# Moving weight sums and one layer norm in a fused attention and MLP kernel on one core

## The chip, the cores and the metric

One NeuronCore of a Trainium2 chip. Times are device microseconds of one execution; a run gives one time, and the median of the runs is compared. A profiled execution is a further run, taken by the hardware profiler.

## What is computed

The input x has 2048 rows of 1024. A layer norm is followed by linear attention with 32 heads of 32 and learned softmax features, and a second layer norm by a dense layer with 3584 hidden columns and a ReLU. All is fp32.

```python
xn = layernorm(x)
q, k, v = split(xn @ wqkv)                      # 32 heads of 32
pq, pk = q @ w_phi, k @ w_phi                   # per head
phi_q = concat(softmax(pq), softmax(-pq)); phi_k = the same of pk
o = (phi_q @ (phi_k.T @ v)) / (phi_q @ sum(phi_k) + 1e-6)
h = x + o @ wo
out = h + relu(layernorm(h) @ w1) @ w2
```

## The kernel before

Every large product is made of groups of three matmuls (`mm3`, lines 182 to 184): high half by high half, high by low, low by high. The halves come from splitting an fp32 tile: ScalarE copies the rounded high half, and VectorE or POOL (GpSimd) subtracts it to get the low half. One group of three is one *step*. The order of the work on each engine is the order in which the program writes it; nothing is reordered later. `when(step, f, ...)` puts a piece of side work right behind the given step of the matmul stream, so an engine's queue runs in order of steps, and an engine that waits holds all that stands behind it. Engines do not wait for the step itself, only for data and buffers, so a queue may also run ahead.

Steps 0 to 255 make keys and values of the first half of the rows in four slabs. Steps 256 to 383 make its queries in two slabs of eight row tiles: slab 0 in steps 256 to 319, slab 1 in 320 to 383. From step 328 on each item of eight steps is followed by two groups of four transposes of a normed row tile of the second half (`ln_turn`, L245). Steps 384 to 639 are keys and values of the second half, 640 to 767 its queries. Steps 768 to 1023 (`wo_first`) are the output projection, with the attention interleaved: unit u goes through products on POOL (`at_sums`, tile ez, L575), sums on VectorE (`at_reduce`, L581), scaling on POOL (`at_scale`, L603 for the first six units, L613 after them), a transpose on VectorE (`at_turn`, L619), and, two units at a time, 128 small matmuls (`at_num`, L633), whose four banks (two named tp, two ac) are then read by ScalarE and by VectorE (`at_low`, L651). In the late part `at_num` comes every 16 steps: ... 894, 910, 926, 942, 958. From step 1024 on the two dense products run.

*Weight units.* `Units` loads weights into six raw tiles (SP's queue, L324 to L337), splits each into a ring of ten (`advance`: ScalarE L125, then L129 on VectorE or POOL) and frees a place when its last step has passed. A slab has eight units. While slab 0 of the queries holds eight places, two of the next slab's units can be split; units 2 to 7 follow as steps 312 to 317 free places. Of these, units 2 and 5 are subtracted on VectorE, 3, 4, 6 and 7 on POOL.

*Weight sums.* The dense products use a seven-multiplication scheme on blocks of 2 by 2, which needs sums and differences of blocks of w1 and w2. They are made early, in 56 pieces. Each piece has a load of 512 KB (`t_load`, L352) seven or fifteen steps ahead, four subtractions on POOL at four consecutive steps (`t_sum`, L362, tiles 128x256), and a store of 512 KB six steps after the first (`t_store`, L365). Loads and stores go through SP's queue. Home 0 is a pair of buffers in the pool tsum, home 1 a pair in the pool fold (closed at step 256), home 2 the two xn tiles of the first layer norm.

*Layer norm ahead of the dense layers.* The kernel's name for it is LN2, and the halves of rows are its first and second part (b = 0 and 1); "first layer norm" in the change's title is b = 0. In each, four pairs of row tiles go through `ln_pair`, 40 steps apart from step 832 on (`wo0 + 64`): stage 0 loads both tiles (L215, tile xin, two buffers), 1 statistics (VectorE, L221), 2 the scale (POOL, L230 to L232), 3 the norm (ScalarE, L238), stages 4, 5 and 6 four transposes each into a tp bank (L245) with ScalarE's copy out (L247), stage 7 four more (L714), ScalarE's copy (L716) and two VectorE operations (L718, L719), stage 8 two POOL subtractions (L724, L725). `ln_store` then stores seven parts from SP (L734, 256 KB each, two to a step): x1's first half, two sums, x1's second half, x2's first half, a further sum (s4), x2's second half. SP's queue also has the attention loads (`at_load`, L543) and the loads and stores of the projection (L658, L687).

Of the kernel before, what the change touches and what calls it, by code (L numbers as in the profile page):

```python
# [140 lines left out]
def kernel(  # L141
# [47 lines left out]
    def do(n, k, f, *args):  # L189
        at[n, k].append((f, args))  # L190
# [663 lines left out]
    def item(gen, *args, keys):  # L854
        items.append((gen, args + (keys,)))
        steps.extend((k,) for k in keys)
        return len(items) - 1
# [11 lines left out]
    for b, tiles in enumerate(groups):  # L869
        for hf in range(2):  # L870

            pairs = b == 0 and hf == 0
            for j in range(0, 4, 2 if pairs else 1):
# [3 lines left out]
                for half in range(2):  # L877
                    n = item(wo_pair, tiles[j:j + 2], hf, half, keys=[("wo", hf, 4 * half + k // 2) for k in range(8)])
# [26 lines left out]
    def when(step, f, *args):  # L905

        if step < 8 * first_up:
            do(step // 8, step % 8, f, *args)
        else:
            do(first_up + (step - 8 * first_up) // 4, step % 4, f, *args)  # L910
# [4 lines left out]
    for t in range(1, NT):  # L915
        n = t - 1 if t < HT else q_n[1, t - HT] + 1
# [131 lines left out]

    LN2 = ((0, 9, 12, 17, 24, 25, 26, 27, 29, 36), (0, 18, 26, 32, 40, 42, 44, 46, 50, 60))
    wo0 = 8 * wo_first
    up0 = 8 * first_up
    for i in range(4):
        for stage in range(9):
            when(wo0 + 64 + 40 * i + LN2[0][stage], ln_pair, 0, i, stage)
            when(up0 + 60 + 68 * i + LN2[1][stage], ln_pair, 1, i, stage)
        for j in range(7):
            when(wo0 + 64 + 40 * i + LN2[0][9] + j // 2, ln_store, 0, i, j)
            when(up0 + 60 + 68 * i + LN2[1][9] + j, ln_store, 1, i, j)  # L1060
    assert wo_n[8, 0] + 10 < first_up

    def up_step(b, p, m):

        return up0 + 4 * (up_n[b, p, m] + 1 - first_up)

    for j, m in enumerate(UP):

        for g in range(2):
            step = up0 + (8 * j + (-62, -32)[g] if j < 4 else 6 * (j - 4) + 10 + 2 * g)  # L1070
# [4 lines left out]
            step = up_step(0, NP - 1, m) + 3 * j  # L1075
# [4 lines left out]
    for b in range(2):  # L1080
# [6 lines left out]


    sixth = 10, 19, 28, 37, 46, 55
    sums_at = [30, 39, 47, 55] + [64 * i + k for i in (1, 2, 3, 4) for k in sixth] + [332, 344, 356, 368] + \  # L1090
        [64 * i + k for i in (6, 7, 8, 9) for k in sixth]
    for n, (w, p, j) in enumerate((w, p, j) for w in (1, 2) for p in range(NP) for j in range(2)):
        step = sums_at[n]
        home = 0 if n % 4 < 2 or 236 < step < 400 else 1 if step < 256 else 2
        when(step - (7 if 256 < step < 400 else 15), t_load, w, p, j, home)
        for k in range(4):
            when(step + k, t_sum, (w, p, j), k)
        when(step + 6, t_store, w, p, j)

    for b in range(2):  # L1100
        for m in DOWN:
            n = down_n[b, m, NP - 1] + 1
# [111 lines left out]
```

## Time and profile before

| | |
|---|---|
| runs, median | 1895.59 us (3 runs, 1893.38 to 1896.5) |
| profiled execution, own time | 1895.65 us |
| its span, first to last instruction | 1893.9 us |
| mean granted TensorE clock | 0.998 |
| TensorE busy | 1879.6 us, 99% of the span |
| VectorE, ScalarE, POOL busy | 1048.3, 740.3, 975.9 us |
| DMA | 432.17 MB, mean 228 GB/s |
| POOL on weight sums (L362) | 176 + 48 subtractions, 144.6 + 41.6 us |

The span is cut into instructions by engine and line. PE is TensorE, DVE VectorE, ACT ScalarE, SP the queue that issues most DMAs. A timeline row has the start, the length, engine, line, operation, tiles, shapes and count; where the engine sat idle before it, brackets give the time and what ended the idle time. Matmuls are pipelined, so the listed length of one (0.39 us) is longer than the distance to the next; distances between starts tell the rate. The chain of waits that ended last is TensorE for 87% of the span and POOL for 7%.

### The profile page before, as it was taken

What the parts mean: (1) busy time and instruction counts of PE and PEld (TensorE: products, weight loads), DVE (VectorE), ACT (ScalarE), POOL (GpSimd) and SP (SyncE); (2) the same over time, 40 slices, a digit from 0 to 9 for tenths busy, and PEclk for the clock granted to TensorE, in tenths of its full rate; (3) what the DMA queues carried; (4) which work ended last, traced back from release to release, by engine and by line L of the source; (5) the groups of instructions that cost most, each with busy time, mean ns of one, the idle gap of its engine ahead of it and who ended that gap; (6) DMA issues with size and microseconds to landing.
All of it is one profiled execution on the core that took longest, in us unless ns stands there. A gap on an engine that the chain in (4) does not pass through costs nothing.

```text
span 1893.9 us, 31847 instructions
## 1 busy us (share of the span) xinstructions
PE 1879.6 (99%) x11640; PEld 1541.0 (81%) x11640; DVE 1048.3 (55%) x1687; ACT 740.3 (39%) x1258; POOL 975.9 (52%) x959
## 2 busy tenths in 40 slices
PE   9999999999999999999999999999999999999999
PEld 7777778888788787888888888888888888888887
DVE  6787668677689776555544563334333433343333
ACT  5322235222233122255454554444444444444442
POOL 4887743888936988323333222222344444444443
PEclk9999999999999999999999999999999999999999
DMA  7888687566555676796877986666677677767775
GB/s 224 289 292 290 228 284 253 187 197 199 186 195 175 205 243 211 251 271 212 276 229 244 296 271 218 184 194 204 216 238 218 197 233 237 240 212 219 215 215 179
DMA packets 292365, 432.17 MB, mean 228 GB/s; under 512 B 24048, under 2 KB 150000, under 8 KB 292208
## 3 DMA queue, kind: packets, MB, share of 16 engines
q1 hardware_dynamic: 275312, 413.36, 68.8%
q10 hardware_dynamic: 16896, 16.78, 2.6%
q8 instruction: 91, 1.49, 0.3%
q14 instruction: 66, 0.54, 0.1%
HBM read 292.68 MB, written 137.36 MB: 227 GB/s over the span
## 4 chain that ended last, share of the span: by engine, by line
PE 87%; POOL 7%; DMA 3%; issue 1%; DVE 1%; SPq 0%; ACT 0%; POOLq 0%; ACTq 0%
PE mm L182 22%; PE mm L183 22%; PE mm L184 22%; PE ac L182 4%; PE ac L184 4%; PE ac L183 4%; PE tp L182 2%; PE tp L184 2%; PE tp L183 2%; POOL ez L575 2%; POOL b L362 1%; PE tp L245 1%; DMA b<-in_w_dram 1%; POOL w L129 1%; POOL qe L613 1%
## 5 line engine op out<-in xcount | busy, mean ns | idle before, releaser
L129 POOL TENSOR_TENSOR w<-raw,w 128x512 fp32r<-128x512 f32 x353 | 468.2, 1328 | 733.1 <-ACT w L125 696.4
L125 ACT ACTIVATE w<-raw 128x512 fp32r<-128x512 f32 x686 | 409.6, 628 | 506.1 <-PE mm L184 249.9
L129 DVE TENSOR_TENSOR w<-raw,w 128x512 fp32r<-128x512 f32 x333 | 272.1, 818 | 525.2 <-ACT w L125 522.0
L182 PE MATMUL mm<-w,xT 128*128 128x512 f32 x768 | 306.4, 399 | 0.0
L183 PE MATMUL mm<-w,xT 128*128 128x512 f32 x768 | 301.5, 393 | 4.1 <-POOL w L129 3.8
L184 PE MATMUL mm<-w,xT 128*128 128x512 f32 x768 | 300.4, 391 | 0.0
L182 PE MATMUL mm<-hT,w 128*128 128x512 f32 x672 | 262.6, 391 | 0.0
L183 PE MATMUL mm<-hT,w 128*128 128x512 f32 x672 | 261.7, 389 | 0.5 <-DVE hT L754 0.5
L184 PE MATMUL mm<-hT,w 128*128 128x512 f32 x672 | 261.6, 389 | 0.0
L183 PEld LDWEIGHTS mm<-w,xT 128*128 128x128 f32 x768 | 144.9, 189 | 34.6 <-POOL w L129 5.6
L362 POOL TENSOR_TENSOR b<-b 128x256 f32<-128x256 f32 x176 | 144.6, 822 | 54.9 <-DMA b<-in_w_dram 44.7
L182 PEld LDWEIGHTS mm<-w,xT 128*128 128x128 f32 x768 | 144.9, 189 | 34.2 <-issue 2.9
L184 PEld LDWEIGHTS mm<-w,xT 128*128 128x128 f32 x768 | 144.9, 189 | 30.9
L182 PE MATMUL mm<-w 128*128 128x512 f32 x392 | 152.5, 389 | 0.0
L183 PE MATMUL mm<-w 128*128 128x512 f32 x392 | 152.5, 389 | 0.0
L184 PE MATMUL mm<-w 128*128 128x512 f32 x392 | 152.5, 389 | 0.0
L183 PEld LDWEIGHTS mm<-hT,w 128*128 128x128 f32 x672 | 126.2, 188 | 26.8 <-DVE hT L754 1.1
L184 PEld LDWEIGHTS mm<-hT,w 128*128 128x128 f32 x672 | 126.2, 188 | 26.3
L182 PEld LDWEIGHTS mm<-hT,w 128*128 128x128 f32 x672 | 126.2, 188 | 25.8
L182 PEld LDWEIGHTS mm<-w 128*128 128x128 f32 x392 | 73.6, 188 | 15.3
L184 PEld LDWEIGHTS mm<-w 128*128 128x128 f32 x392 | 73.6, 188 | 15.3
L183 PEld LDWEIGHTS mm<-w 128*128 128x128 f32 x392 | 73.6, 188 | 15.2
(170 smaller groups left out, 3143.9 us busy)
## 6 DMA issues: line engine op xcount, KB each, us to landing
raw<-t SPq DMA_DIRECT2D x224, 256.0 KB, 3.8
raw<-ad SPq DMA_DIRECT2D x196, 256.0 KB, 3.0
raw<-in_w_dram SPq DMA_DIRECT2D x168, 256.0 KB, 3.0
ad<-c SPq DMA_DIRECT2D x112, 256.0 KB, 3.5
b<-in_w_dram SPq DMA_DIRECT2D x44, 512.0 KB, 5.7
t<-b SPq DMA_DIRECT2D x44, 512.0 KB, 5.0
ad<-s SPq DMA_DIRECT2D x84, 256.0 KB, 4.1
ed<-qe ACTq DMA_DIRECT2D x32, 512.0 KB, 4.3
```

The costliest lines, as they stand in the source:

```text
L125: nc.scalar.activation(w[:, 0, :], raw[1], AF.Copy)
L129: eng.tensor_tensor(out=w[:, 1, :], in0=raw[1], in1=w[:, 0, :].bitcast(F32), op=ALU.subtract)
L182: pe.matmul(ps, a_hi, b_hi, start=first, stop=False, skip_group_check=more)
L183: pe.matmul(ps, a_hi, b_lo, start=False, stop=False, skip_group_check=more)
L184: pe.matmul(ps, a_lo, b_hi, start=False, stop=last, skip_group_check=more)
L245: pe.transpose(pt[:, k, :], xn[:, (4 * j + k) * P:(4 * j + k + 1) * P], ident)
L362: pool.tensor_tensor(out=tsum[*u, *out], in0=tsum[*u, *a], in1=tsum[*u, *b], op=ALU.subtract)
L575: pool.tensor_tensor(out=ez, in0=e_q[u].rearrange("p (i h) s f -> p i (h s f)", i=4)[:, 2 * j:2 * j + 2, :], in1=zb[:, q, None, 256 * r:25 ...
L613: pool.tensor_tensor(out=e, in0=e, in1=sd[:, :, None].to_broadcast([P, 32, 32]), op=ALU.mult)
```

## The change

Three edits to the table of side work. No operation is added or taken out.

1. Steps of the sums (`sums_at`). In steps 256 to 320: six sums at 266, 275, 284, 293, 302, 311 become four at 266, 276, 286, 296. In steps 320 to 384: four at 332, 344, 356, 368 become five at 332, 342, 352, 362, 372. All later sums keep their steps but each is made one place earlier in the list, and the last one goes to step 650, in the first query slab of the second half.
2. Homes of the buffers. Up to step 236 as before (0, 0, 1, 1); from there to 384 home 0; from 394 on the rotation 0, 0, 2, 2 is counted from the sum at 394 (`half_on`).
3. For the second pair (i = 1) of the layer norm with b = 0, stages 4 to 8 come five steps later and the stores one step later: with base step 872, stage 4 goes from 896 to 901, stage 7 from 899 to 904, stage 8 from 901 to 906, the stores from 908 to 909.

```diff
+    NEAR1 = 0, 9, 12, 17, 29, 30, 31, 32, 34, 37
     LN2 = ((0, 9, 12, 17, 24, 25, 26, 27, 29, 36), (0, 18, 26, 32, 40, 42, 44, 46, 50, 60))
...
     for i in range(4):
+        near = NEAR1 if i == 1 else LN2[0]
         for stage in range(9):
-            when(wo0 + 64 + 40 * i + LN2[0][stage], ln_pair, 0, i, stage)
+            when(wo0 + 64 + 40 * i + near[stage], ln_pair, 0, i, stage)
...
         for j in range(7):
-            when(wo0 + 64 + 40 * i + LN2[0][9] + j // 2, ln_store, 0, i, j)
+            when(wo0 + 64 + 40 * i + near[9] + j // 2, ln_store, 0, i, j)
...
     sixth = 10, 19, 28, 37, 46, 55
-    sums_at = [30, 39, 47, 55] + [64 * i + k for i in (1, 2, 3, 4) for k in sixth] + [332, 344, 356, 368] + \
-        [64 * i + k for i in (6, 7, 8, 9) for k in sixth]
+    sums_at = [30, 39, 47, 55] + [64 * i + k for i in (1, 2, 3) for k in sixth] + \
+        [266, 276, 286, 296, 332, 342, 352, 362, 372] + [64 * i + k for i in (6, 7, 8, 9) for k in sixth] + [650]
+    half_on = sums_at.index(64 * 6 + 10)
     for n, (w, p, j) in enumerate((w, p, j) for w in (1, 2) for p in range(NP) for j in range(2)):
         step = sums_at[n]
-        home = 0 if n % 4 < 2 or 236 < step < 400 else 1 if step < 256 else 2
+        home = (0, 0, 1, 1)[n % 4] if step < 236 else (0, 0, 2, 2)[(n - half_on) % 4] if n >= half_on else 0
         when(step - (7 if 256 < step < 400 else 15), t_load, w, p, j, home)
```

## The prediction

> **What bounds the kernel now.** I read the page's busy times first, then the list of TensorE's waits, then the timelines around each wait that the edited steps touch.
>
> ```profile
> PE 1879.6 (99%) x11640; PEld 1541.0 (81%) x11640; DVE 1048.3 (55%) x1687; ACT 740.3 (39%) x1258; POOL 975.9 (52%) x959
> ```
>
> The waits of TensorE (who, for whom: us in all, times, the longest):
>
> ```profile
> PE mm L183 <- POOL w L129: 3.8, 3, 3.2
> ...
> PE tp L245 <- DVE oT L651: 1.2, 1, 1.2
> ```
>
> TensorE is busy 99% of the span, and nothing in the diff removes a matmul. All that scheduling can give is TensorE's waits and what follows them. Two waits stand where the edit works: 3.2 us on POOL's split of a weight unit (L183, matmul with the unit's low half), and 1.2 us of a layer-norm transpose (L245) on VectorE.
>
> The first wait in TensorE's timeline (columns: start, us, engine, line, operation; idle time before it in brackets):
>
> ```profile
> 260.32 0.39 PE L182 MATMUL mm<-w,xT 128*128 128x512 f32 x1
> ...
> 264.40 0.39 PE L182 MATMUL mm<-w,xT 128*128 128x512 f32 x1
> 267.99 0.79 PE L183 MATMUL mm<-w,xT 128*128 128x512 f32 x1 [3.20 <-POOL w L129]
> ...
> 273.49 0.63 PE L182 MATMUL mm<-w,xT 128*128 128x512 f32 x1
> ...
> 274.71 0.40 PE L182 MATMUL mm<-w,xT 128*128 128x512 f32 x1
> ```
>
> From 260.32 to 264.40 there are six steps (18 matmuls): 4.08 / 18 = 0.227 us each, 0.68 a step. From 264.40 to 274.71 there are five steps (15 matmuls), which would take 3.40 us and took 10.31. So this stall costs **6.91 us**, twice its listed wait: the matmuls behind it last 0.63 instead of 0.39 until 274.
>
> What held POOL, by its timeline:
>
> ```profile
> 251.76 3.20 POOL L362 TENSOR_TENSOR b<-b 128x256 f32<-128x256 f32 x4 [3.14 <-DMA b<-in_w_dram]
> 257.97 3.65 POOL L362 TENSOR_TENSOR b<-b 128x256 f32<-128x256 f32 x4 [3.01 <-DMA b<-in_w_dram]
> 264.37 2.34 POOL L362 TENSOR_TENSOR b<-b 128x256 f32<-128x256 f32 x3 [2.75 <-DMA b<-in_w_dram]
> 266.67 1.26 POOL L129 TENSOR_TENSOR w<-raw,w 128x512 fp32r<-128x512 f32 x1
> ...
> 268.58 3.74 POOL L129 TENSOR_TENSOR w<-raw,w 128x512 fp32r<-128x512 f32 x3
> ```
>
> ScalarE's timeline there, the copies that go ahead of POOL's subtractions:
>
> ```profile
> 257.86 3.98 ACT L125 ACTIVATE w<-raw 128x512 fp32r<-128x512 f32 x6 [2.60 <-PE mm L184]
> ```
>
> These three L362 groups are the sums of steps 293, 302 and 311. Each waits for its load, and the load for a store two sums back, as the chain shows:
>
> ```profile
> 242.71 4.05 DMA t<-b
> 246.77 4.85 DMA b<-in_w_dram
> ```
>
> With two buffers, store 4.05, load 4.85, subtractions 3.2 and issue make about 6.3 us a sum (251.76, 257.97, 264.37), against nine steps of 0.68 = 6.1: the sums run late and do not catch up. The sum of step 311 starts at 264.37, and the splits of units 3, 4, 6 and 7 of the second query slab stand behind it in POOL's order. ScalarE had their copies ready from 259.
>
> **The change, part by part.**
>
> *Sums in the early query slabs.* Removed before step 320: two of six sums (302 and 311); the other four go to 266, 276, 286, 296. The loads and stores between keep their order on SP's queue, each held by the landing before it, so the sum of step 296 takes the place of the one at 251.76 and ends at 254.96. POOL is then free. Unit 3's copy is ScalarE's second: 257.86 + 2 x 0.66 = 259.2. Four POOL subtractions of 1.26 end at 260.5, 261.7, 263.0, 264.3. TensorE wants the low halves at 264.63 (264.40 + 0.227), then one, three and four steps later: 265.3, 266.7, 267.4. The smallest margin is 3.1 us. Two units come from VectorE, which has no sum. I take **-6.91 us**; bounds: 0 if POOL is late all the same, -6.91 since no more was lost.
>
> *The five sums from 332 on (four before).* The sums keep their count of instructions and DMAs (56 loads, 224 subtractions, 56 stores); one more falls into steps 332 to 384.
>
> ```profile
> 290.44 3.20 POOL L362 TENSOR_TENSOR b<-b 128x256 f32<-128x256 f32 x4 [2.95 <-DMA b<-in_w_dram]
> 298.77 3.19 POOL L362 TENSOR_TENSOR b<-b 128x256 f32<-128x256 f32 x4 [5.13 <-DMA b<-in_w_dram]
> ...
> 314.50 1.29 POOL L129 TENSOR_TENSOR w<-raw,w 128x512 fp32r<-128x512 f32 x1 [7.20 <-ACT w L125]
> ```
>
> From issue to landing, the sums' loads (view of tile b), then their stores (view of tile t):
>
> ```profile
> DMA to landing us min/median/max: 3.2/5.5/11.0
> DMA to landing us min/median/max: 2.9/3.9/8.9
> ```
>
> A buffer's loop is 5.5 + 3.2 + 3.9 and some 0.5 of issue = 13.1 us, 6.55 a sum with two buffers. Ten steps here last ten times 0.68 plus a transposition of x every eighth step, above 6.8. So the five keep pace. The load for 332 goes out at step 325, two steps after the one that began at 264.40, and behind a load of x: about 266.5. So the fifth ends near 266.5 + 5.5 + 3.2 + 4 x 6.8 = 302.4. The next split is that at 314.50, 307.6 after the stall's removal. POOL's 7.20 us of idle time ahead of it covers the extra sum: 0 us. Without that cover each us over 307.6 plus TensorE's own slack (a rival, below) would count.
>
> *The sum at 650.* Load behind the raw loads of step 635, subtractions behind the last zacc add, store ahead of the attention loads.
>
> ```profile
> 525.88 3.79 POOL L603 TENSOR_TENSOR qe<-qe,smq 128x1024 f32<-128x1024 f32 x2 [5.54 <-DMA qe<-ed]
> 551.80 5.06 POOL L129 TENSOR_TENSOR w<-raw,w 128x512 fp32r<-128x512 f32 x4 [22.13 <-ACT w L125]
> ```
>
> and SP's attention loads:
>
> ```profile
> 520.74 3.04 SPq L543 DMA_DIRECT2D qe<-ed  x4
> ```
>
> Its 3.2 to 3.5 us fit into POOL's 5.54 us of idle time. SP's store waits for them, so the four attention loads go out some 3.4 us later; if their tiles lie where the sum's buffer lay, they wait for the store too, at most 8.9 more. POOL's L603 then slides from 525.88 to at most 538, and 22.13 us of POOL idle time stand behind it. 0 us; without that idle time it would cost its own 3.5. The buffers' rotation begun anew gives each step from 394 on the same kind of buffer as before: 0.
>
> *Second layer-norm pair five steps later.*
>
> ```profile
> 713.66 0.40 PE L184 MATMUL mm<-w,oT 128*128 128x512 f32 x1
> 715.26 0.66 PE L245 MATMUL tp<-ident,xin 128*128 128x128 f32 x4 [1.20 <-DVE oT L651]
> ```
>
> ```profile
> 721.39 1.30 POOL L724 TENSOR_TENSOR s<-s,xin 128x512 f32<-128x512 f32 x1 [1.60 <-DVE xin L719]
> ...
> 724.01 5.00 POOL L575 TENSOR_TENSOR ez<-qe,zb 128x512 f32<-128x512 f32 x4
> ```
>
> The transpose comes 1.60 us after the last matmul instead of one slot of 0.23: 1.37 us lost. It needs a tp bank that the attention matmuls filled two steps before and VectorE empties late. Five steps (3.4 us) later the bank is free: -1.37 there, and full rate is not lost (the matmuls around it last 0.40). But POOL's L724 and L725 (1.30 each) now queue behind the ez products instead of ahead of them (from about 725.8, not 721.39), and on SP the last stores of the pair, which read their results, move past the two attention loads of step 911:
>
> ```profile
> 724.51 0.45 SPq L734 DMA_DIRECT2D hs<-xin  x1
> 725.06 0.41 SPq L734 DMA_DIRECT2D hs<-s4l  x1
> 728.25 0.81 SPq L543 DMA_DIRECT2D qe<-ed  x2
> 729.15 1.15 SPq L734 DMA_DIRECT2D hs<-xin  x1
> 730.35 0.72 SPq L658 DMA_DIRECT2D xh<-in_x_dram  x1
> 731.12 5.73 SPq L215 DMA_DIRECT2D xin<-hd  x2
> ```
>
> The landing of the pair's seven stores (view of tile hs):
>
> ```profile
> DMA to landing us min/median/max: 2.1/2.8/7.4
> ```
>
> Behind them VectorE, POOL and TensorE:
>
> ```profile
> 740.48 1.29 DVE L221 BATCH_NORM_STATS2 st<-xin 128x6 f32<-128x512 f32 x2 [0.51 <-DMA xin<-hd]
> 742.64 1.29 POOL L575 TENSOR_TENSOR ez<-qe,zb 128x512 f32<-128x512 f32 x1 [4.12 <-DVE qtz L581]
> 765.97 1.25 DVE L619 STREAM_TRANSPOSE qe<-qe 128x1024 f32<-128x1024 f32 x1 [0.95 <-POOL qe L613]
> 767.37 0.34 PE L633 MATMUL tp<-qe,kvL 32*32 32x128 f32 x8
> ```
>
> The third pair's second load (the later half of 731.12 + 5.73) reuses a buffer and waits for the store issued at 729.15; VectorE's statistics wait for that load, the sums over ez queue behind them, POOL behind those without a gap from 742.64 on, and the last attention matmuls start at 767.37, only 0.15 us after VectorE's transpose (765.97 + 1.25). So TensorE can be early there only if this chain is. After the change the two stores of 0.45 and 0.41 us and the load of 0.72 precede the last store; that is 1.6 us, less some 0.2 since the two attention loads, held by POOL's result rather than by the attention matmuls, start about as now. If the last store again needs 7.4 us to land behind them, the chain is 1.4 later; with the ordinary 2.8 it is more than 1.4 earlier, and TensorE sets the pace again. I take +1.0, near the first end, because the same two loads stand ahead of that store in both kernels. With the 0.15 us of slack TensorE passes 767.37 later by 0.9: **+0.9 us** for the layer norm instead of -1.37, bounds -1.37 and +1.3 (1.4 less the slack).
>
> Sum: -6.91 + 0.9 = -6.0. The profiled execution took 1895.65 us (span 1893.9), the runs' median is 1895.59, so it is a typical one: 1895.65 - 6.0 = **1889.6 us**.
>
> [...]
>
> **Rivals.**
>
> *The layer norm's gain holds in full*: the third pair's loads land as early as TensorE moves. -6.91 - 1.37 = -8.3: 1887.4 us. For it: ordinary landings are short; against it: the 5.73 row.
>
> *The early stall stays or returns*: POOL is still late at unit 3, or at 386. Then only the layer norm counts, -1.37 to +1.3: 1894.3 to 1897.0, say 1895. Against it: the 3.1 us margin and the 7.20 us of idle time.
>
> *A new wait drops the rate again*: waits of up to 2 us at the attention matmuls near 754 and 767. If one has the tail of the 3.20 us wait (6.91 - 3.20 = 3.7), 1893.3. Against it: the 1.20 us wait at 715.26 had no tail. [...]
>
> *Slower*: the five sums between 332 and 384 overrun the splits of the next units. TensorE needs the split of 307.6 eight steps later, at 313.0. To end 3.8 us above the time before, the loss must be 9.8: a wait of 6.1 and its tail of 3.7. The fifth sum would have to end at 319.1, which is (319.1 - 266.5 - 8.7) / 4 = 11.0 us a sum. With every landing at its maximum it is (11.0 + 3.2 + 8.9) / 2 = 11.55, the fifth sum ends at 266.5 + 14.2 + 4 x 11.55 = 326.9, and the time is 1889.6 + 13.9 + 3.7 = 1907.2. The longest pace in the trace there is 298.77 - 290.44 = 8.3.
>
> **How the numbers follow.** Forecast 0.52, full gain 0.30, stall stays 0.09, lower rate after a new wait 0.05, slower 0.04. A measurement of this kernel tells about 0.2% (3.8 us) from no change, so faster means below 1891.8: the first two, 0.82. The stall that stays and the lower rate end within 3.8 us of 1895.6: same, 0.14. Slower: 0.04. The range holds the first two cases with the runs' spread of about 1 us below 1887.4 and, above, the layer norm's bound (1890.0) and 1 us for each cover costed at nothing but not seen: 1886.4 to 1892.0.
>
> **What would show it.** Right: no L183 wait on POOL near 268 and no 0.63 us matmuls there; the fourth sum ends near 255 and the next L362 stands after 270; L245 without a wait after 715; new waits of L633 on DVE or POOL in the last two attention groups. Wrong: POOL's L362 rows between 300 and 310 with L183 waiting after; L603 later than 550; the third pair's statistics earlier against TensorE than now (then the full gain).

## The result, and the profile after

The changed kernel takes **1889.8 us** (median of 7 runs, 1888.32 to 1891.3) against 1895.59 before (7 runs). The ratio is 0.9971, 95% interval 0.996 to 0.9983: faster by 0.29%. The forecast was 1889.6. The profiled execution has a span of 1888.0 us, 5.9 less than before.

TensorE's waits in the changed kernel (who, for whom: us in all, times, the longest):

```profile
PE tp L245 <- ACT xin L238: 2.4, 1, 2.4
PE tp L245 <- ACT xn L238: 1.6, 1, 1.6
PE tp L1136 <- POOL ones L1132: 1.6, 1, 1.6
PE tp L633 <- DVE qe L619: 0.7, 1, 0.7
...
PE mm L183 <- POOL w L129: 0.3, 1, 0.3
```

Both waits at which the edit aimed are gone: of L183's 3.8 us on POOL 0.3 us are left, elsewhere, and L245 on VectorE is not in the list. Two are new: 2.4 us of a transpose on ScalarE's norm (tile xin, not the xn of the start) and 0.7 us of the attention matmuls on VectorE's transpose.

TensorE's timeline, first where the early stall was, then at the second pair's turn:

```profile
266.58 0.39 PE L182 MATMUL mm<-w,xT 128*128 128x512 f32 x1
...
267.26 0.39 PE L182 MATMUL mm<-w,xT 128*128 128x512 f32 x1
...
709.54 0.40 PE L184 MATMUL mm<-w,oT 128*128 128x512 f32 x1
709.78 0.60 PE L245 MATMUL tp<-ident,xin 128*128 128x128 f32 x4
```

The matmul at 267.26 is the one at 274.71 before. It stands one step of 0.68 behind its neighbour and lasts 0.39. The transposes follow the last matmul after 0.24 us instead of 1.60.

POOL's timeline there and in the next slab:

```profile
252.93 3.18 POOL L362 TENSOR_TENSOR b<-b 128x256 f32<-128x256 f32 x4 [4.48 <-DMA b<-in_w_dram]
258.70 5.97 POOL L129 TENSOR_TENSOR w<-raw,w 128x512 fp32r<-128x512 f32 x4 [2.59 <-ACT w L125]
...
274.40 3.17 POOL L362 TENSOR_TENSOR b<-b 128x256 f32<-128x256 f32 x4 [4.80 <-DMA b<-in_w_dram]
...
303.25 3.19 POOL L362 TENSOR_TENSOR b<-b 128x256 f32<-128x256 f32 x4 [4.37 <-DMA b<-in_w_dram]
307.01 1.30 POOL L129 TENSOR_TENSOR w<-raw,w 128x512 fp32r<-128x512 f32 x1 [0.57 <-ACT w L125]
```

The fourth sum ends at 256.1, and the four splits run from 258.70 on with no sum among them. The five later sums start from 274.40 to 303.25, 7.2 us apart. The fifth ends at 306.44, and of POOL's 7.20 us of idle time ahead of the next split 0.57 are left: the cover was almost used up.

The place of the late sum on POOL:

```profile
513.49 2.37 POOL L362 TENSOR_TENSOR b<-b 128x256 f32<-128x256 f32 x3
521.87 1.92 POOL L603 TENSOR_TENSOR qe<-qe,smq 128x1024 f32<-128x1024 f32 x1 [6.01 <-DMA qe<-ed]
...
544.25 7.57 POOL L129 TENSOR_TENSOR w<-raw,w 128x512 fp32r<-128x512 f32 x6 [17.78 <-ACT w L125]
```

The attention products L603 come 3.5 us later than before (525.88 - 7.5 = 518.4), and 17.78 us of idle time are left behind them.

From the second pair's turn to the end of the attention, POOL, SP, VectorE and TensorE:

```profile
718.15 1.28 POOL L575 TENSOR_TENSOR ez<-qe,zb 128x512 f32<-128x512 f32 x1 [2.42 <-DVE qtz L581]
719.39 1.30 POOL L724 TENSOR_TENSOR s<-s,xin 128x512 f32<-128x512 f32 x1
```

```profile
716.31 0.32 SPq L734 DMA_DIRECT2D hs<-s  x1
717.51 0.32 SPq L687 DMA_DIRECT2D hd<-xh  x1
720.71 0.32 SPq L734 DMA_DIRECT2D hs<-s  x1
721.12 0.38 SPq L734 DMA_DIRECT2D hs<-xin  x1
721.60 0.90 SPq L543 DMA_DIRECT2D qe<-ed  x2
722.55 0.45 SPq L734 DMA_DIRECT2D hs<-xin  x1
723.09 0.38 SPq L734 DMA_DIRECT2D hs<-s4l  x1
723.53 0.86 SPq L658 DMA_DIRECT2D xh<-in_x_dram  x1
724.48 0.62 SPq L734 DMA_DIRECT2D hs<-xin  x1
725.19 6.51 SPq L215 DMA_DIRECT2D xin<-hd  x2
```

```profile
714.43 1.85 DVE L718 TENSOR_TENSOR s<-s,xin 128x512 f32<-128x512 f32 x1 [1.16 <-ACT s L716]
716.20 0.68 DVE L719 TENSOR_TENSOR xin<-xin,s 128x512 f32<-128x512 f32 x1
716.80 0.68 DVE L684 TENSOR_TENSOR xh<-mm,xh 128x512 f32<-128x512 f32 x1
717.40 1.86 DVE L581 TENSOR_REDUCE qtz<-ez 128x16 f32<-128x512 f32 x3
...
735.41 1.29 DVE L221 BATCH_NORM_STATS2 st<-xin 128x6 f32<-128x512 f32 x2 [0.47 <-DMA xin<-hd]
```

```profile
742.02 0.66 PE L245 MATMUL tp<-ident,xin 128*128 128x128 f32 x4 [2.35 <-ACT xin L238]
```

SP stands from 717.83 to 720.71 before the store of POOL's L724, which runs behind the ez products. POOL itself idles 2.42 us before the fourth of these: it waits for the first of VectorE's sums over ez (L581, 717.40), and these stand in VectorE's queue behind the pair's L718 and L719, which the move put there. The two attention loads, the rest of the stores and the third pair's loads all come behind that. The third pair's second load lands at 735.41 (VectorE's statistics start on it). Before it was 740.48; with TensorE 8.9 us earlier, that is 3.9 us later against TensorE. The third pair's own transposes then wait for their norm.

How much earlier TensorE is than in the kernel before, part by part, worked out from the starts of the same matmul (L184 of a step) in two timelines; minus is earlier:

| kernel | to step 320 | 320 to 336 (early stall) | 896 to 912 (second pair) | 912 to 960 (third pair, attention's end) | 960 to the end | sum at the last step |
|---|---|---|---|---|---|---|
| changed | -0.54 | -6.95 | -1.41 | +3.30 | -0.23 | -5.85 |

The start differs from run to run (the wait of L245 on xn was 2.7 us before and 1.6 here).

### The profile page after: what moved, and what is told of

It is laid out like the page before. It is cut to its first block, busy times and chain, and to the rows that moved or that the text cites. A ratio compares the mean times of both kernels' runs of the same rounds, so it can differ in the third digit from the quotient of the medians.

```text
span 1888.0 us, 31850 instructions
## 1 busy us (share of the span) xinstructions
PE 1876.7 (99%) x11640; PEld 1539.7 (82%) x11640; DVE 1052.1 (56%) x1687; ACT 739.7 (39%) x1258; POOL 975.1 (52%) x959
## 4 chain that ended last, share of the span: by engine, by line
PE 91%; POOL 5%; DMA 2%; issue 1%; DVE 1%; SPq 0%; ACT 0%; POOLq 0%; ACTq 0%
PE mm L182 23%; PE mm L183 23%; PE mm L184 23%; PE ac L184 4%; PE ac L182 4%; PE ac L183 4%; PE tp L182 2%; PE tp L184 2%; PE tp L183 2%; POOL ez L575 2%; PE tp L245 1%; POOL qe L613 1%; PE ac L464 1%; DMA xin<-hd 1%; POOL w L129 0%
## 5 line engine op out<-in xcount | busy, mean ns | idle before, releaser
L183 PE MATMUL mm<-w,xT 128*128 128x512 f32 x768 | 299.9, 390 | 0.6 <-POOL w L400 0.4
L184 PE MATMUL mm<-w,xT 128*128 128x512 f32 x768 | 299.3, 390 | 0.0
L183 PE MATMUL mm<-hT,w 128*128 128x512 f32 x672 | 261.6, 389 | 0.3 <-DVE hT L754 0.3
L184 PE MATMUL mm<-hT,w 128*128 128x512 f32 x672 | 261.6, 389 | 0.0
L184 PEld LDWEIGHTS mm<-w,xT 128*128 128x128 f32 x768 | 144.2, 188 | 30.6
L183 PEld LDWEIGHTS mm<-w,xT 128*128 128x128 f32 x768 | 144.3, 188 | 29.9 <-POOL w L400 1.0
L183 PE MATMUL mm<-w 128*128 128x512 f32 x392 | 152.5, 389 | 0.0
L184 PE MATMUL mm<-w 128*128 128x512 f32 x392 | 152.5, 389 | 0.0
L183 PEld LDWEIGHTS mm<-hT,w 128*128 128x128 f32 x672 | 126.2, 188 | 26.7 <-DVE hT L754 0.8
L184 PEld LDWEIGHTS mm<-hT,w 128*128 128x128 f32 x672 | 126.2, 188 | 26.3
L184 PEld LDWEIGHTS mm<-w 128*128 128x128 f32 x392 | 73.6, 188 | 15.3
L183 PEld LDWEIGHTS mm<-w 128*128 128x128 f32 x392 | 73.6, 188 | 15.2
```

Source lines behind the costliest of these rows:

```text
L183: pe.matmul(ps, a_hi, b_lo, start=False, stop=False, skip_group_check=more)
L184: pe.matmul(ps, a_lo, b_hi, start=False, stop=last, skip_group_check=more)
```

## The experiments

All are edits of the changed kernel's tables, unless said otherwise, and compute the same. The ratio is to the kernel before, on the same chip, with its 95% interval. The table continues the one above: its last four columns are of one profiled execution each. That of stores_ahead (1892.82 us) is the slowest of its runs, those of five_sums (1888.73) and subs_first (1886.42) are the fastest of theirs, and that of ln_only (1895.19) lies 2.1 us below the median.

| kernel | median us (before, same chip) | ratio | 320 to 336 | 896 to 912 | 912 to 960 | last step |
|---|---|---|---|---|---|---|
| after_again | 1889.78 (1894.52) | 0.9975 (0.9966 to 0.9984) | -6.95 | -1.39 | +2.92 | -6.45 |
| sums_only | 1887.54 (1893.84) | 0.9964 (0.9952 to 0.9975) | -6.93 | -1.00 | 0.00 | -7.52 |
| ln_only | 1897.28 (1893.84) | 1.001 (1.0002 to 1.0019) | -0.75 | -1.41 | +2.16 | -0.48 |
| five_sums | 1890.11 (1893.84) | 0.9981 (0.9972 to 0.999) | -6.95 | -1.41 | +2.23 | -6.92 |
| stores_ahead | 1890.46 (1893.84) | 0.9982 (0.9974 to 0.9991) | -6.95 | -1.41 | +6.31 | -2.84 |
| subs_first | 1887.76 (1894.52) | 0.9968 (0.9955 to 0.998) | -6.95 | -1.39 | +0.23 | -9.27 |
| two_later | 1886.77 (1894.52) | 0.9961 (0.9949 to 0.9974) | -6.95 | -1.39 | +0.04 | -9.44 |
| two_later_again | 1887.04 (1894.83) | 0.9964 (0.9952 to 0.9977) | -6.95 | -1.17 | 0.00 | -8.62 |
| sums_stats | 1887.71 (1894.52) | 0.9966 (0.9954 to 0.9979) | -6.95 | -0.61 | 0.00 | -8.67 |
| two_stats | 1886.76 (1894.83) | 0.9966 (0.9952 to 0.9979) | -6.95 | -1.07 | 0.00 | -8.00 |
| six_ten | 1893.48 (1894.83) | 0.9993 (0.9984 to 1.0002) | -4.32 | -1.41 | +3.72 | -1.90 |
| last_at_636 | 1892.00 (1894.83) | 0.999 (0.9981 to 0.9999) | -6.95 | -1.41 | +3.20 | -3.62 |

**The standard.** The changed kernel, run again beside others. 

> The changed kernel unchanged, as the standard for its neighbours. Both theories: 5 to 6 us below the kernel before; TensorE 6.9 us earlier at step 336, 1.4 more at 912, and 2 to 3.3 us lost between 936 and 960.


Measured: as expected. The loss of the third pair was 2.9 us here and 3.3 in the first profile; the two executions differ by 0.4 us.

**The two parts alone.**

```diff
-    NEAR1 = 0, 9, 12, 17, 29, 30, 31, 32, 34, 37
+    NEAR1 = 0, 9, 12, 17, 24, 25, 26, 27, 29, 36     # sums_only
```

> The changed kernel with the second pair of the layer norm put back to its old steps (stage 4 at 896, stores from 908). Theory: the sums' new places save the whole early stall, 6.9 us, and the layer norm's move gave 1.4 us at its own turn and took 3.3 us back later (2.56 at the third pair's turn, 0.75 at the last attention matmuls), because the pair's last store goes behind two attention loads on SP's queue. So here the 1.2 us wait of L245 near 708 is back, the 2.35 us wait of L245 on ScalarE's norm near 742 is gone, and the time is 1889.8 - 1.9 = 1887.9 us. Rival: the wait near 742 comes from the sums' earlier stream or from a slow DMA, not from the move; then it stays here, and the time is 1891 us.


Measured: 1887.54, near the theory's 1887.9. No wait at the third pair or the last attention matmuls. The 1.2 us wait at the second pair's turn did not come back in full: 0.2 us is left.

```profile
PE tp L245 <- DVE oT L651: 0.2, 1, 0.2
```

With the sums moved, that wait was 0.2 us here and 0.6 in sums_stats below. Whether the execution or the sums' earlier stream makes it shorter than 1.2 was not separated.

ln_only keeps the sums' table and homes of the kernel before and has the layer norm's move. 

> The kernel before with the layer norm's move alone; sums and homes as before. Theory: the early stall of 6.9 us stays, the move costs 1.9 us net: 1897.5 us, with the wait of L245 on ScalarE's norm (2 to 2.5 us) at the third pair's turn. Rival: the move alone is worth its 1.4 us: 1894.2 us and no such wait.


Measured: slower than before, by little more than the noise: 1.001 (1.0002 to 1.0019). The early stall stays, the second pair gains 1.41, the third pair and the last attention lose 2.16. The third pair's wait is 1.2 us, not the expected 2 to 2.5, and the move costs 0.75 us net in this execution, not 1.9. The two parts together show that the sums carry the whole gain and that the layer norm's move takes part of it back.

**Which order makes the third pair late, SP's or POOL's.** First the stores earlier:

```diff
-    NEAR1 = 0, 9, 12, 17, 29, 30, 31, 32, 34, 37
+    NEAR1 = 0, 9, 12, 17, 29, 30, 31, 32, 34, 35     # stores_ahead
```

> The changed kernel with the second pair's seven stores two steps earlier (from 907 on), so that the last one goes out at step 910, ahead of the two attention loads of step 911. POOL's order is that of the changed kernel. Theory (SP's order makes the third pair late): the store lands in its ordinary 2 to 3 us, the third pair's second load lands some 3 us earlier against TensorE, the waits near 742 and 762 vanish, and the attention loads, 1 to 2 us later, are covered: 1889.8 - 3.3 = 1886.5 us. Rival (POOL's late subtractions L724 and L725 make it late, whatever the order on SP): the store still waits for them, a wait of at least 1 us stays at the third pair's turn, 1888.5 us or above.


Measured: in the profiled execution the third pair's turn waits 3.3 us, not less but more, and the half-rate tail is there:

```profile
742.89 1.12 PE L245 MATMUL tp<-ident,xin 128*128 128x128 f32 x4 [3.31 <-ACT xin L238]
743.65 0.78 PE L182 MATMUL mm<-w,oT 128*128 128x512 f32 x1
744.23 0.63 PE L183 MATMUL mm<-w,oT 128*128 128x512 f32 x1
```

That execution is the slowest of eleven, so a typical one loses less; but none took under 1889.91 us, and the theory wanted 1886.5. My theory of SP's order fell. The last store did land 2.9 us earlier against TensorE (23.0 us after step 895 for 25.9 in the changed kernel). But the third pair's second load then took 7.9 us instead of 4.0 and landed 1.0 us later; why it took longer is open. With the stores ahead, SP waits for POOL's subtraction with still more behind it. What stays is POOL's result. Next it was made earlier:

```diff
-    NEAR1 = 0, 9, 12, 17, 29, 30, 31, 32, 34, 37
+    NEAR1 = 0, 9, 12, 17, 29, 30, 31, 32, 32, 37     # subs_first
```

> The changed kernel with stage 8 of the second pair (POOL's L724 and L725) at step 904 instead of 906, so that they stand in POOL's order ahead of the second half of the ez products (unit 27, step 905), not behind it. Stores as in the changed kernel, the last one still behind the attention loads of step 911. Theory, as it stands after the run with the stores ahead: POOL's late result holds SP at the pair's third store, and all loads behind it bunch up. Here the result comes 2.4 us sooner, so do the attention loads and the third pair's loads, and the wait of L245 at the third pair's turn falls below 0.5 us: 2 us faster than the changed kernel. Rival (SP's order of the last store behind two loads): that order stays, so does the wait of 1.3 to 2.4 us.


Measured: 1887.76, 2.0 us faster than after_again on the same chip; in the profiled execution the wait at the third pair is gone, with SP's order as in the changed kernel. POOL's timeline of subs_first:

```profile
715.47 1.30 POOL L724 TENSOR_TENSOR s<-s,xin 128x512 f32<-128x512 f32 x1 [1.54 <-issue]
```

TensorE passes step 896 0.4 us earlier here than in the changed kernel, so L724 runs 3.5 us earlier against it (715.47 against 719.39).

**A smaller move.**

```diff
-    NEAR1 = 0, 9, 12, 17, 29, 30, 31, 32, 34, 37
+    NEAR1 = 0, 9, 12, 17, 26, 27, 28, 29, 29, 36     # two_later
```

> The changed kernel with the second pair's turn two steps later than before instead of five (stage 4 at 898), stage 8 at 901 and stores from 908 as before. Theory: the bank is free at 898, or nearly, and POOL and SP keep their old order, so the third pair's loads land as in the kernel before: TensorE gains 1.0 to 1.4 us at the second pair's turn and gives it back only at the last attention matmuls if VectorE's chain is late there: 2 to 3 us faster than the changed kernel. Rival (any later turn makes the third pair late): the wait of 1.3 us or more at the third turn stays.

> The kernel with the second pair's turn two steps later once more, beside its neighbours: 2 to 3 us faster than the changed kernel, 0.4% faster than the kernel before.


Measured: 1886.77 and 1887.04, the fastest of all with two_stats. two_later is 3.0 us faster than after_again on the same chip, and no run of the one reaches a run of the other. Two steps sufficed for the bank: -1.39 and -1.17 us at the turn, and no wait of L245 on VectorE. Against the sums alone (1887.5, and 1887.7 in sums_stats) the gain is under 1 us, the runs overlap, and it is not settled. In two_later stage 8 keeps its place in POOL's order ahead of the ez products:

```profile
713.75 1.30 POOL L724 TENSOR_TENSOR s<-s,xin 128x512 f32<-128x512 f32 x1 [2.02 <-DVE xin L719]
715.13 1.28 POOL L725 TENSOR_TENSOR s4l<-xin,s 128x512 f32<-128x512 f32 x1
716.38 5.01 POOL L575 TENSOR_TENSOR ez<-qe,zb 128x512 f32<-128x512 f32 x4
```

**The third pair's statistics out of VectorE's way.** sums_stats has the layer norm as before but, for i = 2, `0, 14, 15, 17, 24, 25, 26, 27, 29, 36`; two_stats has that and two_later's table. 

> The sums' change alone, with the third pair's statistics, scale and norm put behind VectorE's sums over ez (steps 926, 927, 929 instead of 921, 924, 929), so that a late load of that pair no longer holds VectorE's queue and with it the attention chain. Theory (that hold sets the pace of the last attention matmuls): POOL's 4 to 6 us of idle time before the fourth ez product goes, the last transpose of VectorE ends 3 us ahead of TensorE's last attention matmuls, no wait of L633 there; the time is that of the sums alone or up to 1 us better. Rival: the third pair's turn becomes late itself by its later statistics, a wait of L245 near step 936 of 1 us or more, and the time is that of the changed kernel.

> The sums' change, the second pair's turn two steps later with stage 8 and the stores as before, and the third pair's statistics, scale and norm at 926, 927, 929. Theory: the second pair's turn keeps its 1.3 us, and VectorE is no longer held by the third pair's load; but in the run with the turn two steps later no wait was left at the third pair or at the last attention matmuls, so this adds nothing: equal to that run within 0.5 us in the trace. Rival: TensorE still loses time to the third pair, up to 1 us faster.


Measured: the gap on POOL is gone (sums_stats, four ez products in a row, 5.04 us),

```profile
726.48 5.04 POOL L575 TENSOR_TENSOR ez<-qe,zb 128x512 f32<-128x512 f32 x4
```

and no wait is left from 912 to 960, but none was left in sums_only and two_later either. sums_stats ties with sums_only, two_stats with two_later.

**How many sums, and where in POOL's order.**

```diff
-        [266, 276, 286, 296, 332, 342, 352, 362, 372] + ...
+        [266, 275, 284, 293, 302, 332, 344, 356, 368] + ...                   # five_sums
+        [266, 276, 286, 296, 306, 316, 332, 344, 356, 368] + ...              # six_ten, without the sum at 650
```

> The changed kernel with five sums in steps 256 to 320, nine steps apart as before (266, 275, 284, 293, 302), then four as before (332, 344, 356, 368) and the last at 650. Theory: only what stands in POOL's order ahead of unit 3's split counts; the fifth sum ends at 261.6 in the frame of the kernel before, the four splits at 262.9, 264.1, 265.4, 266.7 against needs at 264.6, 265.3, 266.7, 267.4: no wait, TensorE as early at step 336 as in the changed kernel (-6.9), time 1889.8 us. Rival: nine steps apart the sums lose ground and five already stall TensorE; a wait of 1 to 3 us with its half-rate tail near 265, 1893 to 1896 us.


Measured: no wait near step 323, -6.95 as in the changed kernel. One sum less was enough, nine steps apart. 

> The changed kernel with all six sums kept in steps 256 to 320, ten steps apart (266 to 316), then four (332, 344, 356, 368) and none at 650. Theory (what counts is what stands ahead of a unit's split in POOL's order, not how many sums there are): the sixth sum's load still lands near 264.4 in the frame of the kernel before, but at step 316 the sum stands behind the splits of units 3 and 4 and around those of 6 and 7, which end near 266.4 and 268.4 against needs at 266.7 and 267.4: a wait of about 1 us without a half-rate tail, TensorE 5.5 to 6.9 us earlier at step 336 than in the kernel before. Rival (six sums are two too many for POOL and the landings): the stall of 3 us and its tail stay, TensorE gains under 2 us at step 336.


Measured: -4.32, between the two expectations and nearer the theory's. POOL's order is the expected one, the splits of two units ahead of the sixth sum and two between its subtractions:

```profile
258.24 3.94 POOL L362 TENSOR_TENSOR b<-b 128x256 f32<-128x256 f32 x4 [2.79 <-DMA b<-in_w_dram]
262.14 2.53 POOL L129 TENSOR_TENSOR w<-raw,w 128x512 fp32r<-128x512 f32 x2
265.00 0.73 POOL L362 TENSOR_TENSOR b<-b 128x256 f32<-128x256 f32 x1 [0.32 <-DMA b<-in_w_dram]
265.69 1.26 POOL L129 TENSOR_TENSOR w<-raw,w 128x512 fp32r<-128x512 f32 x1
```

The splits of units 6 and 7 end at 266.95 and 268.87. TensorE is 0.88 us ahead of the kernel before in this execution, so that is 1.4 us later than reckoned, and three short waits (0.15, 0.62 and 0.95 us, 1.72 together) go with a loss of 2.6 us, without a tail. As a whole six_ten is no faster than the kernel before (0.9993, 0.9984 to 1.0002): it also has the layer norm's loss, 3.72 us in this execution.

**The late sum in a worse place.**

```diff
-        ... for k in sixth] + [650]
+        ... for k in sixth] + [636]     # last_at_636
```

> The changed kernel with the last sum at step 636 instead of 650: its four subtractions then stand in POOL's order among the splits for which TensorE already waits 0.3 us at step 647. Theory (the place at 650 is free because POOL idles behind it): here two to four of the 0.75 to 0.9 us subtractions come ahead of unit 7's split, the wait at step 647 grows by 1.5 to 3.5 us, and with it comes the half-rate tail if it passes some 2.5 us: 1.5 to 7 us slower than the changed kernel at step 656. Rival: the sums are covered anywhere near there; no change.


Measured: TensorE loses 1.8 us between steps 640 and 656, two waits of 0.52 and 1.40 us without a tail (the matmuls behind them last 0.50, then 0.39 and 0.40 us). The 2.5 us of the expectation was my estimate, between a wait of 2.35 us without a tail (changed kernel) and one of 2.57 us with it (ln_only); no run shows such a limit, and the 1.88 us of six_ten, told at the end, speaks against it. The place at 650 is free because POOL idles behind it, not because four subtractions are nothing.

## Why the prediction was right, and where it was not

*The early stall* (-6.91): measured -6.95, in ten of the twelve other runs to 0.02. The cause is shown: five_sums and six_ten change what stands ahead of the splits in POOL's order, and the stall goes with that, not with the count of the sums alone (six in six_ten) or their distance alone (nine steps in five_sums).

*The five sums from 332 on* (0): right in the sum, but the cover was overrated. The forecast had the fifth sum end at 302.4; it ended at 306.4. The first one began at 274.4 and not at 272.0, since its load went out at 267.75 and took 6.5 us, and a sum took 7.2 us and not 6.8. By the prediction's reckoning 5.4 us of TensorE's own slack stood behind that.

*The sum at 650* (0): right; the loads moved by 3.2 us and L603 by 3.5, as worked out, and last_at_636 shows the price without the cover.

*The layer norm* (-1.37 at the turn, +0.9 in all, bounds to +1.3): the mechanism was right, the gain given back through the third pair's loads, but in the changed kernel the size fell outside the bounds and the place was off. The term that was too small is "the chain is 1.4 later", of which the forecast took +1.0. L724 was expected 12.8 us after step 895 and ran at 13.9, the last store went out at 19.0 instead of the 17.8 reckoned, and the load landed 2.45 us later than before, not 1.0. The 1.1 us of L724 come from VectorE, by the wait for the fourth ez product shown above: L718 and L719 took 1.85 and 0.68 us here, and 0.69 each before:

```profile
719.96 0.69 DVE L718 TENSOR_TENSOR s<-s,xin 128x512 f32<-128x512 f32 x1 [3.07 <-ACT s L716]
720.57 0.69 DVE L719 TENSOR_TENSOR xin<-xin,s 128x512 f32<-128x512 f32 x1
```

In all seven runs in which L724 stands behind the ez products, it ran 11.4 us plus the lengths of these two after step 895. Where both took 0.69 (ln_only), it ran at 12.8, as forecast, and the load landed 1.3 us later; in five_sums, with 1.36 and 0.68, 1.4 later. In these two profiles the move cost 0.75 and 0.82 us net, inside the bounds. In the changed kernel the third pair and the attention's end lost 3.30 us, net +1.89 (+1.53 in after_again, +1.79 in last_at_636, +2.31 with a stretch at half rate in six_ten). The first to wait was not an attention matmul but the third pair's own transposes, whose norm hangs on the same load. And the order to blame was POOL's more than SP's: stores_ahead refuted SP's order as the one cause, subs_first showed POOL's.

*The sum*: -6.0 predicted. The parts measured -6.95 and +1.89, that is -5.06; the rest of the -5.85 is the start (-0.54) and the end (-0.23), which change from execution to execution. The forecast agreed with the median to 0.2 us partly by that luck: the layer norm was 1.0 us off.

*The rivals.* The full gain (1887.4) is what two_later reaches, and the sums alone nearly (1887.5). A new wait that drops the rate did not come in the changed kernel (2.35 us, then 0.39 us matmuls) but did in stores_ahead (3.31 us, then 0.63) and six_ten (1.88 us, 0.63 somewhat later). The slower case did not come near: the five sums stood 7.2 us apart on average, against 11.0.

## What to carry to other kernels

Where an engine's queue is in program order, ask what stands ahead of the instruction that the busy engine awaits; one sum fewer there was worth as much as two (-6.95 us in five_sums and in the changed kernel). A step that is moved by more than its wait needs carries its other engines' work past other queues: two steps were enough for TensorE (-1.39 us at the turn in two_later), five (-1.41) put POOL's part behind 5 us of products, and VectorE's ahead of the sums that these products wait for, and gave the gain back (+3.30 us behind it). And follow the buffer that the moved work frees to its next user, and from there to the first wait on TensorE.

## What the runs showed of the hardware that I had not expected

TensorE's half rate did not go by the length of the wait alone. After waits of 2.57 us (ln_only), 3.20 (before) and 3.31 (stores_ahead) the rows of L184 behind them lasted 0.63 us at once, and the mean granted clock of each of these executions is 0.998. After 1.20 (before) and 2.35 us (changed kernel) they lasted 0.40. The changed kernel's mean clock is 1.000, and so is that of last_at_636, which has a wait of 2.3 us. But in six_ten (0.999) a wait of 1.88 us was followed, 2 us later, by a stretch at half rate:

```profile
743.87 0.66 PE L245 MATMUL tp<-ident,xin 128*128 128x128 f32 x4 [1.88 <-ACT xin L238]
...
746.22 0.63 PE L183 MATMUL mm<-wf,oT 128*128 128x512 f32 x1
```

The trace of the kernel before shows a granted clock of 0.50 from 267.79 to 274.62 us, that is 6.83 us, and of 1.00 from 4.97 us to there and from there to 1890. In the trace of the changed kernel it is 1.00 from 7 to 1886 us, with the wait of 2.35 us among them. From the first matmul of 0.63 us to the next of 0.40 it was 6.13 us in the kernel before (268.58 to 274.71), 6.04 in ln_only (267.16 to 273.20) and 2.48 in six_ten (746.22 to 748.70). Why 1.88 us was followed by the half rate in six_ten, and 2.35 us in the changed kernel was not, is open.

Not every execution of the kernel before lost as much: of the 65 timed beside the experiments four have a mean granted clock of 1.000, and they took 1889.9 to 1891.7 us, the others, at 0.997 to 0.999, 1894.5 in the median.

VectorE's L718 took 1.85 us in the changed kernel while POOL worked on ez products (714.43 us), and 0.69 us in the kernel before while POOL was idle (719.96 us). In these two traces, up to 800 us, seven instructions of L718 and L719 had no two-input operation of POOL beside them and took 0.68 or 0.69 us; the nine that had one took 1.14 to 1.85. That POOL's work slows them was not tried by itself.
